# Banded attention with a gated feed-forward: probabilities transposed by VectorE blocks and a DMA round trip instead of TensorE

## The chip, the cores and the metric

The kernel runs on one core of a Trainium2 chip. A core has TensorE (matmuls into PSUM), VectorE (DVE), ScalarE (ACT), GpSimd (POOL), and SyncE (SP), which here issues all DMAs. The metric is device time in microseconds (us), the median over runs of the whole program.

## The reference

Inputs are q, k, v of shape 4 x 8 x 768 x 64 (batch, heads, positions, head size) and four weight matrices. All is float32.

```python
scores = scale * np.matmul(q, k.transpose(0, 1, 3, 2))
rel = pos[:, None] - pos[None, :]
is_global = pos[None, :] < int(n_global)              # 8
is_local = (rel >= 0) & (rel < int(n_local))          # 96
keep = is_global | is_local
dist = np.where(is_global & ~is_local, float(n_local), np.abs(rel))
scores = np.where(keep, scores - slopes * dist, -1000000000.0)
a = softmax(scores)                                   # with 1e-9 added to the sum
attn = np.matmul(a, v)                                # 3072 rows of 512
a = x @ w1                                            # x: attn, heads side by side
b = x @ w2
h = a * b @ w3
out = h @ w_out
```

So each query sees 8 global keys and up to 96 keys behind it, and the result of all heads goes through a gated feed-forward without nonlinearity.

## The kernel before

**Tiling.** The 768 positions of a sequence are cut into 3 blocks of T = 256 rows (`NCB`), 12 blocks in all (`c`), each with two row tiles of 128 (`j`, `NQ` = 2). Heads go in pairs (`hp`, 4 of them; `u` is the head in the pair). A step `s` handles two head pairs of one block (`STEP` = 2), so there are n = 24 steps, two to a block. For one row tile and head the keys are a window of 104 (96 before the tile and the 8 global ones) and the tile's own 128, together 232 columns. On the first block of a sequence the tile j = 0 has no window.

**A step.** `scores` (L406) makes the scores of both pairs in PSUM, 32 small matmuls. `rows` (L421, L422) adds the bias and takes the row maximum on VectorE and does exp with the row sum on ScalarE. `softmax` (L427 to L436) scales the rows by the reciprocal sum, one head on ScalarE, the other on VectorE. `flip` (L445, L447) transposes one row tile's probabilities of both heads on TensorE, four 128x128 transposes against an identity (two where there is no window), and copies the PSUM bank to the tile `ph` on ScalarE (L449); a step has four flips. `values` (L457, L459) multiplies them by v in the next step. `split` (L63, L64) cuts the result into a high and a low part, the tiles `xh` and `xl`, so that the feed-forward can run as three matmuls of the type float32r.

**Feed-forward.** `w3` and `w_out` are multiplied together once at the start (L142). `FeedForward.run` is a generator of slices of about six matmuls of 512 columns (L161 to L163 for the two gates, L178 to L180 for the output). A block of work is appended to the list `work` when its last attention result has been split (blocks 0 and 1 alone, then two blocks together, 48 slices). `slices(k)` emits the next k slices of that list.

**Order.** The order on TensorE and, from step 4 on, on ScalarE is that of the program text; on VectorE and SyncE it is that of the text in steps 0 to 3 only, and the scheduler's after that. From step 4 on a step stands as follows in the text: `visit` (values of the step before, scores of this one, split of the step before), rows, two slices, softmax, the loads of the next step, more slices, and then four flips with slices between them by the table `SLICES`:

```python
SLICES = [()] * 3 + [(4, 2, 2, 1, 1)] * 3 + [(4, 2, 1, 1, 1)] * 2 + [(5, 2, 2, 2, 1)] * (n - 8)
```

**Buffers.** PSUM: the scores have four banks, the flips one, the values one, the feed-forward (`ps_m`) two. `ph` has four buffers of one row tile each, `pr` (probabilities) two, the output tile `ot` two. SyncE issues the loads `qr` (L384) and `vr` (L391) and the stores of the output (L185) in its one queue.

The function `dense` (L207 to L311) is a second path for other band widths, behind a condition; it does not run here.

Of the kernel before, what the change touches and what calls it, by code (L numbers as in the profile page):

```python
# [39 lines left out]
W = 2 * T  # L40
# [20 lines left out]
def split(nc, hi, lo, x):  # L61

    nc.scalar.activation(hi, x, AF.Copy)  # L63
    nc.vector.tensor_tensor(out=lo, in0=x, in1=hi.bitcast(F32), op=ALU.subtract)  # L64
# [142 lines left out]
def dense(ctx, tc, ff, nf, ident, qk, vx):  # L207

    nc = tc.nc
    NB = S // P  # L210
    dr = ctx.enter_context(tc.tile_pool(name="dr", bufs=1, space=bass.MemoryType.DRAM))
    xs = dr.tile([B, NCB, P, NP, T], F32, name="xs")
    with tc.tile_pool(name="dm", bufs=1) as dm, tc.tile_pool(name="dw", bufs=1) as dw, tc.tile_pool(name="dp", bufs=1, space=PSUM) as dp:

        nv = dm.tile([P, 2], F32, name="nv")
        for i in range(2):
            lo, hi = nf[:, 2 * i:2 * i + 1], nf[:, 2 * i + 1:2 * i + 2]
            n = nv[:, i:i + 1]
# [3 lines left out]
        ng, nl = nv[:, 0:1], nv[:, 1:2]  # L222
        far = dm.tile([P, 1], F32, name="far")
        nc.vector.tensor_scalar(out=far, in0=nl, scalar1=0.0, scalar2=None, op0=ALU.max)
        for qb in range(NB):
# [17 lines left out]
            with tc.For_i(0, B, 1) as b:  # L243
                for h in range(H):
                    hp, u = divmod(h, 2)
                    nm = f"{qb}_{h}"
                    src = qk[bass.ds(b, 1), cq, hp, u * D:(u + 1) * D, KW + jq * P:KW + (jq + 1) * P]
                    qd = dw.tile([P, P], F32, tag="qd", name=f"qd_{nm}")
                    kd = dw.tile([P, NB, P], F32, tag="kd", name=f"kd_{nm}")
                    vd = dw.tile([P, NB, D], F32, tag="vd", name=f"vd_{nm}")  # L250
                    for g in range(2):
                        rows = slice(g * D, (g + 1) * D)
                        nc.sync.dma_start(out=qd[rows], in_=src[0])
                        for i in range(NB):
# [5 lines left out]
                    kh = dw.tile([P, NB * P], F32R, tag="kh", name=f"dkh_{nm}")  # L260
                    kl = dw.tile([P, NB * P], F32R, tag="kl", name=f"dkl_{nm}")
                    vs = dw.tile([P, NB, 2, D], F32R, tag="vs", name=f"dvs_{nm}")
# [24 lines left out]
                    ph = dw.tile([P, NB, 2, P], F32R, tag="ph", name=f"dph_{nm}")  # L287
                    for i0 in range(0, NB, 4):
                        i1 = min(i0 + 4, NB)
# [5 lines left out]
                    for i in range(NB):  # L295
                        nc.tensor.matmul(pv, lhsT=vs[:, i], rhs=ph[:, i], start=i == 0, stop=i == NB - 1)
# [28 lines left out]
def banded(ctx, tc, ff, ns, nt, nf, oki, ident, qk, vx):  # L325
# [17 lines left out]
    biasw = bp.tile([P, H, UW], BF16, name="biasw")  # L343

    def biases():
        it = at.tile([P, UW], I32, tag="ph", bufs=4, name="it")
        itg = at.tile([P, P], I32, tag="ph", bufs=4, name="itg")
# [46 lines left out]
    def scores(c, hp, qr):  # L394

        ps = sc[hp % STEP]
        for j in range(NQ):
            w0 = BW if c % NCB == 0 and j == 0 else 0  # L400
            for g in range(P // HQ):
                cols = slice(max(w0, g * HQ), BW + (g + 1) * HQ)
                q0 = KW + j * P + g * HQ
                for u in range(2):
                    m = qr[u * D:(u + 1) * D]
                    nc.tensor.matmul(ps[u][g * HQ:(g + 1) * HQ, j, cols], lhsT=m[:, q0:q0 + HQ], rhs=m[:, j * SLOT:][:, cols], start=True, stop=True)  # L406
        return ps
# [28 lines left out]
                    nc.vector.tensor_scalar(out=x, in0=x, scalar1=r, scalar2=None, op0=ALU.mult)  # L436
        return pr

    def flip(c, hp, j, pr):

        first = c % NCB == 0 and j == 0
        nk = 1 if first else 2
        pt = ps_t.tile([P, 2, 2, P], F32, tag="t", name=f"t_{c}_{hp}_{j}")
        for u in range(2):
            nc.tensor.transpose(pt[:, u, 0], pr[:, j, u, BW:UW], ident)  # L445
            if not first:
                nc.tensor.transpose(pt[:, u, 1], pr[:, j, u, 0:P], ident)  # L447
        ph = at.tile([P, 2, 2, P], F32, tag="ph", bufs=4, name=f"ph_{c}_{hp}_{j}")
        nc.scalar.activation(ph[:, :, :nk], pt[:, :, :nk], AF.Copy)  # L449
        return ph  # L450

    def values(uu, c, hp, vr, phs):
        for j, ph in enumerate(phs):
            first = c % NCB == 0 and j == 0
            for u in range(2):
                rows, o = slice(u * D, (u + 1) * D), uu[u * D:(u + 1) * D, j * P:(j + 1) * P]
                nc.tensor.matmul(o, lhsT=vr[:, j, rows], rhs=ph[:, u, 0], start=True, stop=first)  # L457
                if not first:
                    nc.tensor.matmul(o, lhsT=vr[:BW, 2 * NQ - 1 - j, rows], rhs=ph[:BW, u, 1], start=False, stop=True)  # L459

# [7 lines left out]
    def slices(k):  # L468
        while k > 0 and work:
            if next(work[0], "end") == "end":  # L470
                work.pop(0)
            else:
                k -= 1

    def loads(s, keys=True, vals=True):
        if s < n and keys:
            qrs[s] = [load(*p) for p in pairs(s)]
        if s < n and vals:
            vrs[s] = [load_values(*p) for p in pairs(s)]

    def visit(s):
        if s:
            c, h0 = pairs(s - 1)[0]
            if h0 == 0 and c % 2 == 0:
                xs[c // 2] = [xp.tile([P, NCC, W], F32R, tag=tag, name=f"{tag}_{c}") for tag in ("xh", "xl")]
            uu = ps_v.tile([P, STEP, T], F32, tag="v", name=f"v_{c}_{h0}")
            for i, p in enumerate(pairs(s - 1)):
                values(uu[:, i], *p, vrs[s - 1][i], phs[s - 1][NQ * i:NQ * (i + 1)])
        ps = [scores(*p, t) for p, t in zip(pairs(s), qrs[s])] if s < n else []
        if s:  # L490
            x2 = xs[c // 2]
            xc = [x[:, :, c % 2 * T:][:, :, :T] for x in x2]
            split(nc, *(x[:, h0:h0 + STEP] for x in xc), uu)
            if h0 + STEP == NP and c < 2:
                work.append(ff.run(c, *xc, c * T, T))
            elif h0 + STEP == NP and c % 2:
                work.append(ff.run(c, *x2, (c - 1) * T, W))
        return ps

    def all_rows(s, ps):  # L500
        return [rows(*p, x) for p, x in zip(pairs(s), ps)]

    def turn(s, m, prs):
        phs.setdefault(s, []).append(flip(*pairs(s)[m // NQ], m % NQ, prs[m // NQ][0]))

    def first_steps():

# [94 lines left out]
        fits(nc, ff.mp, nf, oki)  # L602


    SLICES = [()] * 3 + [(4, 2, 2, 1, 1)] * 3 + [(4, 2, 1, 1, 1)] * 2 + [(5, 2, 2, 2, 1)] * (n - 8)
    with tc.manual_schedule(engines={mybir.EngineType.PE}):
        with tc.manual_schedule(engines={mybir.EngineType.DVE, mybir.EngineType.SP}):
            first_steps()
        with tc.manual_schedule(engines={mybir.EngineType.Activation}):
            for s in range(4, n + 1):  # L610
                rs = all_rows(s, visit(s))
                if s == n:
                    break

                slices(2)
                for p, r in zip(pairs(s), rs):
                    softmax(*p, *r, nc.vector)
                loads(s + 1)
                slices(SLICES[s][0] - 2)
                for m in range(STEP * NQ):  # L620
                    turn(s, m, rs)
                    slices(SLICES[s][m + 1])
            slices(10 ** 6)


# [43 lines left out]
```

## Time and profile before

| | |
|---|---|
| median of 3 runs | 600.2 us (599.47 to 601.7) |
| profiled execution: span of its instructions | 597.9 us; of its time outside the span nothing is on record |
| TensorE busy | 574.8 us, 96% |
| VectorE, ScalarE busy | 261.2 us, 287.3 us |
| transposes on TensorE | 192 of L445, 160 of L447 |
| copies of their PSUM bank on ScalarE (L449) | 96, 560 ns each |
| granted TensorE clock, mean | 0.997 |
| DMA | 54.01 MB, mean 90 GB/s |

A row of the groups reads: line, engine, operation, output tile <- input tiles, shapes and count, then busy us and mean ns of one, then the idle time of the engine just before, with what ended it. A row of the timeline reads: start us, duration us, engine, line, operation, tiles, and count where rows are merged. Ends of matmuls are modelled, so starts are the safer reading. In the rows of DMA issues the last number is the median us from issue to landing. In the rows of DMA queues stand packets, MB, and the packets' time as a share of 16 DMA engines over the stretch.

### The profile page before, as it was taken

To read this page: it belongs to the slowest core of one execution; us is meant where nothing else is said; L and a number is where in the kernel's file an instruction comes from. 1 tells how busy PE (TensorE), PEld (TensorE's weight loads), DVE (VectorE), ACT (ScalarE), POOL (GpSimd) and SP (SyncE) were. 2 spreads that over 40 slices of the span, in tenths; PEclk is the share of its full clock that TensorE was granted. 3 is DMA by queue.
4 is the path that set the end of the run, shared out by engine and by line. 5 is a ranking of instruction groups with operands and counts; after the bars stand their busy time and mean duration, and the time that the engine had idled before them with its cause. 6 is when DMAs were issued, how large, how long until landed. Compare 5 with 4: busy or idle time off the path is not lost.

```text
span 597.9 us, 9930 instructions
## 1 busy us (share of the span) xinstructions
PE 574.8 (96%) x3872; PEld 456.3 (76%) x3872; DVE 261.2 (44%) x851; ACT 287.3 (48%) x777; POOL 1.3 (0%) x10
## 2 busy tenths in 40 slices
PE   2998998999999999999999999999999999999995
PEld 0444568989988888888888888888888888888884
DVE  8999998531434425304533322542343453112200
ACT  3065667644556456435635545653553663422210
POOL 0000000000000000000000000000000000000000
PEclk9999999999999999999999999999999999999998
DMA  8896654220132202212211320220331120000011
GB/s 304 296 362 235 218 207 145 81 81 29 52 96 97 77 3 79 81 37 81 79 43 36 115 98 18 62 64 2 123 105 37 42 80 19 36 18 1 0 37 40
DMA packets 23240, 54.01 MB, mean 90 GB/s; under 512 B 2704, under 2 KB 4752, under 8 KB 23184
## 3 DMA queue, kind: packets, MB, share of 16 engines
q1 hardware_dynamic: 23184, 53.29, 26.2%
q8 instruction: 32, 0.52, 0.4%
q14 instruction: 24, 0.20, 0.1%
HBM read 46.99 MB, written 6.29 MB: 89 GB/s over the span
## 4 chain that ended last, share of the span: by engine, by line
PE 84%; DVE 10%; DMA 3%; ACT 1%; issue 0%; SPq 0%; DVEq 0%; ACTq 0%
PE m L161 15%; PE m L163 14%; PE m L162 14%; PE o L178 8%; PE o L180 7%; PE o L179 7%; PE s L406 4%; PE v L457 4%; PE t L445 3%; PE v L459 3%; PE t L447 3%; PE w L142 2%; DVE t L56 1%; DVE t L58 1%; DMA stage<-w3t 1%; DMA raws<-w 1%
## 5 line engine op out<-in xcount | busy, mean ns | idle before, releaser
L422 ACT ACTIVATE pr<-pr,mx 128x232 f32<-128x232 f32 (+1 forms) x192 | 88.4, 462 | 48.1 <-DVE mx L421 48.1
L449 ACT ACTIVATE ph<-t 128x512 f32<-128x512 f32 (+1 forms) x96 | 53.7, 560 | 88.3 <-PE t L447 81.1
L171 DVE TENSOR_TENSOR g<-m,a 128x512 f32<-128x512 f32 x48 | 33.2, 691 | 133.4 <-PE m L163 132.7
L161 PE MATMUL m<-xh,w1h 128*128 128x512 f32 (+1 forms) x224 | 84.5, 377 | 0.0
L161 PE MATMUL m<-xh,w2h 128*128 128x512 f32 (+1 forms) x224 | 83.0, 371 | 0.5 <-ACT a L168 0.5
L163 PE MATMUL m<-xh,w2l 128*128 128x512 f32 (+1 forms) x224 | 80.7, 360 | 0.0
L163 PE MATMUL m<-xh,w1l 128*128 128x512 f32 (+1 forms) x224 | 80.6, 360 | 0.0
L162 PE MATMUL m<-xl,w1h 128*128 128x512 f32 (+1 forms) x224 | 80.5, 360 | 0.0
L162 PE MATMUL m<-xl,w2h 128*128 128x512 f32 (+1 forms) x224 | 80.5, 359 | 0.0
L178 PE MATMUL o<-wh,gh 128*128 128x512 f32 x192 | 78.2, 407 | 0.0
L180 PE MATMUL o<-wh,gl 128*128 128x512 f32 x192 | 75.2, 392 | 0.0
L179 PE MATMUL o<-wl,gh 128*128 128x512 f32 x192 | 75.0, 390 | 0.0
L142 PE MATMUL w<-wo,t 128*128 128x512 f32 x128 | 60.7, 619 | 12.3 <-DVE wo L58 11.2
L64 DVE TENSOR_TENSOR xl<-v,xh 128x512 fp32r<-128x512 f32 x24 | 16.6, 690 | 122.5 <-ACT xh L63 122.5
L63 ACT ACTIVATE gh<-g 128x512 fp32r<-128x512 f32 x48 | 30.3, 630 | 68.0 <-DVE g L171 67.2
L142 PEld LDWEIGHTS w<-wo,t 128*128 128x128 f32 x128 | 24.0, 197 | 39.9 <-issue 21.7
L421 DVE CUSTOM_DVE_ANT_0 pr<-s,biasw 128x232 f32<-128x232 f32 x160 | 53.4, 394 | 0.0
L445 PE MATMUL t<-ident,pr 128*128 128x128 f32 x192 | 45.9, 274 | 4.0 <-ACT pr L434 3.4
L161 PEld LDWEIGHTS m<-xh,w1h 128*128 128x128 f32 x224 | 42.2, 189 | 8.5 <-issue 3.3
L161 PEld LDWEIGHTS m<-xh,w2h 128*128 128x128 f32 x224 | 42.3, 189 | 7.0 <-issue 0.7
L163 PEld LDWEIGHTS m<-xh,w1l 128*128 128x128 f32 x224 | 42.2, 189 | 6.6
L163 PEld LDWEIGHTS m<-xh,w2l 128*128 128x128 f32 x224 | 42.2, 189 | 6.5
(84 smaller groups left out, 807.0 us busy)
## 6 DMA issues: line engine op xcount, KB each, us to landing
qr<-qk SPq DMA_DIRECT2D x32, 312.0 KB, 4.2
vr<-vx SPq DMA_DIRECT2D x32, 256.0 KB, 3.1
stage<-w3t SPq DMA_DIRECT2D x15, 512.0 KB, 6.2
out_dram<-ot SPq DMA_DIRECT2D x24, 256.0 KB, 2.0
raws<-w SPq DMA_DIRECT2D x10, 512.0 KB, 5.6
qr<-qk SPq DMA_DIRECT2D x16, 260.0 KB, 3.5
vr<-vx SPq DMA_DIRECT2D x16, 192.0 KB, 2.6
stage<-w SPq DMA_DIRECT2D x6, 512.0 KB, 6.8
```

The source lines that it names most:

```text
L142: nc.tensor.matmul(ps, lhsT=self.t3[f, z][:, i * P:(i + 1) * P].bitcast(F32), rhs=self.wo[:, k].bitcast(F32), start=k == 0, stop=k == NFC - 1)
L161: nc.tensor.matmul(ps[:, z], lhsT=mh, rhs=xh[:, i], start=i == 0, stop=False)
L162: nc.tensor.matmul(ps[:, z], lhsT=mh, rhs=xl[:, i], start=False, stop=False)
L163: nc.tensor.matmul(ps[:, z], lhsT=ml, rhs=xh[:, i], start=False, stop=i == NCC - 1)
L171: nc.vector.tensor_tensor(out=g, in0=ps, in1=a, op=ALU.mult)
L178: nc.tensor.matmul(ps, lhsT=gh[:, f, ts], rhs=self.wh[:, f], start=f == 0, stop=False)
L179: nc.tensor.matmul(ps, lhsT=gh[:, f, ts], rhs=self.wl[:, f], start=False, stop=False)
L180: nc.tensor.matmul(ps, lhsT=gl[:, f, ts], rhs=self.wh[:, f], start=False, stop=f == NFC - 1)
L421: nc.vector.tensor_tensor_reduce(out=pr[:, j, u, w0:], in0=ps[u][:, j, w0:UW], in1=bias, scale=-SCALE, scalar=3.0e38, op0=ALU.add, op1=ALU ...
L422: nc.scalar.activation(pr[:, j, u, w0:], pr[:, j, u, w0:], AF.Exp, bias=m, scale=-1.0, accum_out=sm[:, j, u:u + 1])
L445: nc.tensor.transpose(pt[:, u, 0], pr[:, j, u, BW:UW], ident)
L449: nc.scalar.activation(ph[:, :, :nk], pt[:, :, :nk], AF.Copy)
```

## The change

From step 4 on (`SWAP`) the probabilities are not transposed on TensorE. After `softmax`, `swap` transposes each 32x32 block by itself on VectorE (four instructions of 128x512 a step), stores the tile of a head pair, 512 KB, to device memory, and `back` reads it again in four DMAs of 128 KB that bring each block to its place; the pieces of these loads are 128 floats long. `values` reads the tile with the block order of that layout. In the first block of a sequence GpSimd clears the part without a window. The PSUM copies of the flips go with the flips. Steps 0 to 3 keep the flips, into a tile for both row tiles; the pool's two buffers of the new tile take the place of four of half the size.

The order on TensorE from step 4 on: scores of the step, then values of the step before, then all slices of the step in one run (`SLICES` now holds one number a step: 10, 9, 9, 8 in steps 4 to 7 where there were 10, 10, 9, 9, then 12 as before). The split of the step before (`take`) stands on ScalarE between the rows of the two head pairs. After the last step the values of step 23 stand ahead of what is left of the slices. The renaming in `dense` (`NB` to `NKB`) changes nothing there.

```diff
+BK = 32
+NB = P // BK
+SWAP = 4
...
+    dr = ctx.enter_context(tc.tile_pool(name="dr", bufs=2 * STEP, space=bass.MemoryType.DRAM))
...
-    def flip(c, hp, j, pr):
+    def flip(c, hp, j, pr, ph):
...
-        ph = at.tile([P, 2, 2, P], F32, tag="ph", bufs=4, name=f"ph_{c}_{hp}_{j}")
-        nc.scalar.activation(ph[:, :, :nk], pt[:, :, :nk], AF.Copy)
-        return ph
+        nc.scalar.activation(ph[:, NQ * j:NQ * j + 2, :nk], pt[:, :, :nk], AF.Copy)
+
+    def swap(c, hp, pr):
+        first = c % NCB == 0
+        x = at.tile([P, 2, NB, NQ * 2, BK], F32, tag="ph", name=f"ph_{c}_{hp}")
+        d = dr.tile([NB, BK, 2, NB, NQ * 2 * BK], F32, tag="d", name=f"d_{c}_{hp}")
+        units = pr.rearrange("p j u k -> p (j u) k")
+        if first:
+            nc.gpsimd.memset(x[:, 1, :, :2], 0.0)
+        for k, k0 in ((0, BW), (1, 0)):
+            u0 = 2 if first and k else 0
+            nc.vector.transpose(x[:, k, :, u0:], units[:, u0:, k0:k0 + P].rearrange("p u (b c) -> p b u c", c=BK))
+        nc.sync.dma_start(out=d.rearrange("a r k b e -> (a r) k b e"), in_=x.rearrange("p k b u c -> p k b (u c)"))
+        return x, d
+
+    def back(x, d):
+        for b in range(NB):
+            nc.sync.dma_start(out=x[b * BK:(b + 1) * BK].rearrange("r k a u c -> r k a (u c)"), in_=d[:, :, :, b].rearrange("a r k e -> r k a e"))
...
-    SLICES = [()] * 3 + [(4, 2, 2, 1, 1)] * 3 + [(4, 2, 1, 1, 1)] * 2 + [(5, 2, 2, 2, 1)] * (n - 8)
+    SLICES = [()] * 3 + [(4, 2, 2, 1, 1)] + [10, 9, 9, 8] + [12] * (n - 8)
...
-            for s in range(4, n + 1):
-                rs = all_rows(s, visit(s))
-                if s == n:
-                    break
-
+            for s in range(4, n):
+                ps = all_scores(s)
+                uu = spread(s - 1)
+                rs = []
+                for i, p in enumerate(pairs(s)):
+                    rs.append(rows(*p, ps[i]))
+                    if i == 0:
+                        take(s - 1, uu)
                 slices(2)
+                loads(s + 1)
+                xd = []
                 for p, r in zip(pairs(s), rs):
                     softmax(*p, *r, nc.vector)
-                loads(s + 1)
-                slices(SLICES[s][0] - 2)
-                for m in range(STEP * NQ):
-                    turn(s, m, rs)
-                    slices(SLICES[s][m + 1])
+                    xd.append(swap(*p, r[0]))
+                for x, d in xd:
+                    back(x, d)
+                phs[s] = [x for x, _ in xd]
+                slices(SLICES[s] - 2)
+            take(n - 1, spread(n - 1))
             slices(10 ** 6)
```

`spread` is the values part of the old `visit`, `take` its split and the appending of feed-forward work, `all_scores` its scores.

More of the change, by code (lines that the diff above doesn't have):

```diff
@@ L209, in dense @@
     nc = tc.nc
-    NB = S // P
-    dr = ctx.enter_context(tc.tile_pool(name="dr", bufs=1, space=bass.MemoryType.DRAM))
+    NKB = S // P
+    dr = ctx.enter_context(tc.tile_pool(name="dx0", bufs=1, space=bass.MemoryType.DRAM))
     xs = dr.tile([B, NCB, P, NP, T], F32, name="xs")
@@ L224, in dense @@
         nc.vector.tensor_scalar(out=far, in0=nl, scalar1=0.0, scalar2=None, op0=ALU.max)
-        for qb in range(NB):
+        for qb in range(NKB):
             cq, jq = divmod(qb, NQ)
@@ L248, in dense @@
                     qd = dw.tile([P, P], F32, tag="qd", name=f"qd_{nm}")
-                    kd = dw.tile([P, NB, P], F32, tag="kd", name=f"kd_{nm}")
-                    vd = dw.tile([P, NB, D], F32, tag="vd", name=f"vd_{nm}")
+                    kd = dw.tile([P, NKB, P], F32, tag="kd", name=f"kd_{nm}")
+                    vd = dw.tile([P, NKB, D], F32, tag="vd", name=f"vd_{nm}")
                     for g in range(2):
@@ L253, in dense @@
                         nc.sync.dma_start(out=qd[rows], in_=src[0])
-                        for i in range(NB):
+                        for i in range(NKB):
                             k0 = BW + i % NQ * SLOT
@@ L259, in dense @@
                     qs = dw.tile([P, P], F32R, tag="qs", name=f"dqs_{nm}")
-                    kh = dw.tile([P, NB * P], F32R, tag="kh", name=f"dkh_{nm}")
-                    kl = dw.tile([P, NB * P], F32R, tag="kl", name=f"dkl_{nm}")
-                    vs = dw.tile([P, NB, 2, D], F32R, tag="vs", name=f"dvs_{nm}")
+                    kh = dw.tile([P, NKB * P], F32R, tag="kh", name=f"dkh_{nm}")
+                    kl = dw.tile([P, NKB * P], F32R, tag="kl", name=f"dkl_{nm}")
+                    vs = dw.tile([P, NKB, 2, D], F32R, tag="vs", name=f"dvs_{nm}")
                     nc.scalar.activation(qs, qd, AF.Copy)
@@ L286, in dense @@
                     nc.vector.tensor_scalar(out=t, in0=t, scalar1=sm, scalar2=None, op0=ALU.mult)
-                    ph = dw.tile([P, NB, 2, P], F32R, tag="ph", name=f"dph_{nm}")
-                    for i0 in range(0, NB, 4):
-                        i1 = min(i0 + 4, NB)
+                    ph = dw.tile([P, NKB, 2, P], F32R, tag="ph", name=f"dph_{nm}")
+                    for i0 in range(0, NKB, 4):
+                        i1 = min(i0 + 4, NKB)
                         pt = dp.tile([P, 4, P], F32, tag="t", name=f"dpt_{nm}_{i0}")[:, :i1 - i0]
@@ L294, in dense @@
                     pv = dp.tile([P, 2, P], F32, tag="v", name=f"dv_{nm}")
-                    for i in range(NB):
-                        nc.tensor.matmul(pv, lhsT=vs[:, i], rhs=ph[:, i], start=i == 0, stop=i == NB - 1)
+                    for i in range(NKB):
+                        nc.tensor.matmul(pv, lhsT=vs[:, i], rhs=ph[:, i], start=i == 0, stop=i == NKB - 1)
                     e = dw.tile([P, P], F32, tag="e", name=f"de_{nm}")
@@ L345, in biases @@
     def biases():
-        it = at.tile([P, UW], I32, tag="ph", bufs=4, name="it")
-        itg = at.tile([P, P], I32, tag="ph", bufs=4, name="itg")
+        it = at.tile([P, UW], I32, tag="ph", name="it")
+        itg = at.tile([P, P], I32, tag="ph", name="itg")
         rel, loc = (at.tile([P, UW], F32, tag="pr", name=n) for n in ("rel", "loc"))
@@ L447, in flip, with values @@
                 nc.tensor.transpose(pt[:, u, 1], pr[:, j, u, 0:P], ident)
-        ph = at.tile([P, 2, 2, P], F32, tag="ph", bufs=4, name=f"ph_{c}_{hp}_{j}")
-        nc.scalar.activation(ph[:, :, :nk], pt[:, :, :nk], AF.Copy)
-        return ph
-    def values(uu, c, hp, vr, phs):
-        for j, ph in enumerate(phs):
+        nc.scalar.activation(ph[:, NQ * j:NQ * j + 2, :nk], pt[:, :, :nk], AF.Copy)
[14 more added lines that the diff above has]
+            nc.sync.dma_start(out=x[b * BK:(b + 1) * BK].rearrange("r k a u c -> r k a (u c)"), in_=d[:, :, :, b].rearrange("a r k e -> r k a e"))
+    def values(uu, c, hp, vr, ph, swapped):
+        for j in range(NQ):
             first = c % NCB == 0 and j == 0
             for u in range(2):
+                m = NQ * j + u
+                own, win = (ph[:, 0, :, m], ph[:BW, 1, :, m]) if swapped else (ph[:, m, 0], ph[:BW, m, 1])
                 rows, o = slice(u * D, (u + 1) * D), uu[u * D:(u + 1) * D, j * P:(j + 1) * P]
-                nc.tensor.matmul(o, lhsT=vr[:, j, rows], rhs=ph[:, u, 0], start=True, stop=first)
+                nc.tensor.matmul(o, lhsT=vr[:, j, rows], rhs=own, start=True, stop=first)
                 if not first:
-                    nc.tensor.matmul(o, lhsT=vr[:BW, 2 * NQ - 1 - j, rows], rhs=ph[:BW, u, 1], start=False, stop=True)
+                    nc.tensor.matmul(o, lhsT=vr[:BW, 2 * NQ - 1 - j, rows], rhs=win, start=False, stop=True)
     n = NC * NP // STEP
@@ L479, in loads, with spread, take, all_scores @@
             vrs[s] = [load_values(*p) for p in pairs(s)]
+    def spread(s):
+        c, h0 = pairs(s)[0]
+        if h0 == 0 and c % 2 == 0:
+            xs[c // 2] = [xp.tile([P, NCC, W], F32R, tag=tag, name=f"{tag}_{c}") for tag in ("xh", "xl")]
+        uu = ps_v.tile([P, STEP, T], F32, tag="v", name=f"v_{c}_{h0}")
+        for i, p in enumerate(pairs(s)):
+            values(uu[:, i], *p, vrs[s][i], phs[s][i], s >= SWAP)
+        return uu
+    def take(s, uu):
+        c, h0 = pairs(s)[0]
+        x2 = xs[c // 2]
+        xc = [x[:, :, c % 2 * T:][:, :, :T] for x in x2]
+        split(nc, *(x[:, h0:h0 + STEP] for x in xc), uu)
+        if h0 + STEP == NP and c < 2:
+            work.append(ff.run(c, *xc, c * T, T))
+        elif h0 + STEP == NP and c % 2:
+            work.append(ff.run(c, *x2, (c - 1) * T, W))
+    def all_scores(s):
+        return [scores(*p, t) for p, t in zip(pairs(s), qrs[s])]
     def visit(s):
+        uu = spread(s - 1) if s else None
+        ps = all_scores(s)
         if s:
[L483 to L497, printed above, removed]
+            take(s - 1, uu)
         return ps
@@ L503, in turn @@
     def turn(s, m, prs):
-        phs.setdefault(s, []).append(flip(*pairs(s)[m // NQ], m % NQ, prs[m // NQ][0]))
+        i, j = divmod(m, NQ)
+        c, hp = pairs(s)[i]
+        if j == 0:
+            phs.setdefault(s, []).append(at.tile([P, NQ * 2, 2, P], F32, tag="ph", name=f"ph_{c}_{hp}"))
+        flip(c, hp, j, prs[i][0], phs[s][i])
     def first_steps():
@@ L609, in banded @@
         with tc.manual_schedule(engines={mybir.EngineType.Activation}):
-            for s in range(4, n + 1):
-                rs = all_rows(s, visit(s))
-                if s == n:
-                    break
+            for s in range(4, n):
+                ps = all_scores(s)
+                uu = spread(s - 1)
+                rs = []
+                for i, p in enumerate(pairs(s)):
+                    rs.append(rows(*p, ps[i]))
+                    if i == 0:
+                        take(s - 1, uu)
                 slices(2)
+                loads(s + 1)
+                xd = []
                 for p, r in zip(pairs(s), rs):
                     softmax(*p, *r, nc.vector)
-                loads(s + 1)
-                slices(SLICES[s][0] - 2)
-                for m in range(STEP * NQ):
-                    turn(s, m, rs)
-                    slices(SLICES[s][m + 1])
+                    xd.append(swap(*p, r[0]))
[4 more added lines that the diff above has]
+            take(n - 1, spread(n - 1))
             slices(10 ** 6)
```

## The prediction

> **What bounds the kernel now.** I read the page first: the busy shares, the clock row, the chain that ended last.
>
> ```profile
> span 597.9 us, 9930 instructions
> PE 574.8 (96%) x3872; PEld 456.3 (76%) x3872; DVE 261.2 (44%) x851; ACT 287.3 (48%) x777; POOL 1.3 (0%) x10
> PEclk9999999999999999999999999999999999999998
> PE 84%; DVE 10%; DMA 3%; ACT 1%; issue 0%; SPq 0%; DVEq 0%; ACTq 0%
> PE m L161 15%; PE m L163 14%; PE m L162 14%; PE o L178 8%; PE o L180 7%; PE o L179 7%; PE s L406 4%; PE v L457 4%; PE t L445 3%; PE v L459 3%; PE t L447 3%; PE w L142 2%; DVE t L56 1%; DVE t L58 1%; DMA stage<-w3t 1%; DMA raws<-w 1%
> ```
>
> TensorE is 96% busy at full clock and 84% of the ending chain; the rest is the weight stage at the start. From step 4 on nothing else ends a wait that matters. So PE time taken out comes off the end, unless a new wait opens. Then the timeline of TensorE gives the period of a step (score matmuls to score matmuls) and its parts:
>
> ```profile
> 309.46 0.71 PE L457 MATMUL v<-ph,vr 128*64 128x128 f32 x8
> 310.98 1.37 PE L406 MATMUL s<-qr 64*64 64x168 f32 x32
> 312.28 0.50 PE L161 MATMUL m<-xh,w1h 128*128 128x512 f32 x1
> ...
> 332.71 1.37 PE L406 MATMUL s<-qr 64*64 64x168 f32 x32
> ```
>
> ```profile
> 311.00:332.70 21.70, 21.70 (x153) 17.84 (x152) 8.49 (x30) 11.34 (x30) 0.00 (x0) 1.00 0.19 61
> ```
>
> The last row is that stretch in the view by windows: busy time of PE, PEld, DVE, ACT and POOL, then clock and DMA. TensorE is busy in all of it, VectorE 8.5 us, ScalarE 11.3. The period is 332.71 - 310.98 = 21.73 us: values 1.5 us (309.46 to 310.98), scores 1.3 us, the rest is twelve feed-forward slices and four flips.
>
> **What is removed.** Matmul ends are modelled, so I price a flip by starts, not durations:
>
> ```profile
> 509.66 0.39 PE L180 MATMUL o<-wh,gl 128*128 128x512 f32 x1
> ...
> 512.38 0.39 PE L180 MATMUL o<-wh,gl 128*128 128x512 f32 x1
> 512.61 0.27 PE L445 MATMUL t<-ident,pr 128*128 128x128 f32 x1
> 512.72 0.27 PE L447 MATMUL t<-ident,pr 128*128 128x128 f32 x1
> ...
> 512.97 0.48 PE L178 MATMUL o<-wh,gh 128*128 128x512 f32 x1
> 513.28 0.39 PE L179 MATMUL o<-wl,gh 128*128 128x512 f32 x1
> ...
> 515.82 0.27 PE L445 MATMUL t<-ident,pr 128*128 128x128 f32 x1
> ...
> 519.01 0.27 PE L445 MATMUL t<-ident,pr 128*128 128x128 f32 x1
> ```
>
> Twelve undisturbed matmuls take 512.38 - 509.66 = 2.72 us (0.227 each). A flip and twelve matmuls take (519.01 - 512.61)/2 = 3.20. So a flip costs 0.48 us: four transposes 0.11 apart, then a slow first matmul (0.31 to the next instead of 0.23). Steps 4 to 23 have 80 flips; in the six steps on the first block of a sequence (6, 7, 12, 13, 18, 19) the j = 0 flips, 12 in all, hold two transposes, 0.48 - 2 x 0.11 = 0.26. Removed: 68 x 0.48 + 12 x 0.26 = 35.7 us, all on the bound engine. The period falls to 21.73 - 4 x 0.48 = 19.8 us.
>
> ScalarE loses the PSUM copies below, four a step. It is not the bound: no gain by itself.
>
> ```profile
> L449 ACT ACTIVATE ph<-t 128x512 f32<-128x512 f32 (+1 forms) x96 | 53.7, 560 | 88.3 <-PE t L447 81.1 <-PE t L445 7.1
> L64 DVE TENSOR_TENSOR gl<-g,gh 128x512 fp32r<-128x512 f32 x48 | 33.2, 692 | 31.9 <-ACT gh L63 31.9
> L54 DVE TENSOR_SCALAR t<-stage 128x512 int32<-128x512 int32 x15 | 5.8, 417 | 0.5 <-PE w L142 0.5
> L63 ACT ACTIVATE gh<-g 128x512 fp32r<-128x512 f32 x48 | 30.3, 630 | 68.0 <-DVE g L171 67.2
> ```
>
> **What is added.** VectorE gets four block transposes of 128x512 a step. No row shows one; the nearest of that size are 0.42 us (one source) and 0.69 us (two sources). I take 0.69, since a shuffle across lanes is unlikely to beat a plain pass: 2.8 us a step. With its 8.5 us it has room; the cost is latency. The GpSimd clear on first blocks stands beside TensorE's work: nothing. SyncE gets ten DMAs a step (two stores of 512 KB, eight loads of 128 KB).
>
> The round trip is a new wait of the value matmuls. Time from the first score matmul of a step, by these rows:
>
> ```profile
> 312.33 0.39 DVE L421 CUSTOM_DVE_ANT_0 pr<-s,biasw 128x232 f32<-128x232 f32 x1
> 314.56 0.39 DVE L421 CUSTOM_DVE_ANT_0 pr<-s,biasw 128x232 f32<-128x232 f32 x1
> 312.82 0.49 ACT L422 ACTIVATE pr<-pr,mx 128x232 f32<-128x232 f32 x1 [1.13 <-DVE mx L421]
> 316.14 0.47 ACT L422 ACTIVATE pr<-pr,mx 128x232 f32<-128x232 f32 x1
> 317.09 1.62 ACT L434 ACTIVATE pr<-pr,sm 128x232 f32<-128x232 f32 x4
> ```
>
> Maxima are 0.32 apart ((314.56 - 312.33)/7), exps 0.47 apart. Scores end at 1.3, values at about 3.0. The first pair's maxima start at about 1.0, its exps run 1.5 to 3.4; then `take`'s copy, 0.6, waits for the values and ends at 4.0; the second pair's exps end at 5.9. Two slices end on TensorE at 3.0 + 12 x 0.227 = 5.7; if the second closes a feed-forward block, its product (0.69) and copy (0.63) stand next on ScalarE until about 7.2. The scalings take 1.6: first pair done 8.0, second 8.8. Two transposes each: 9.4 and 10.8. Behind them:
>
> ```profile
> out_dram<-ot SPq DMA_DIRECT2D x24, 256.0 KB, 2.0
> stage_xl<-w3t SPq DMA_DIRECT2D x1, 512.0 KB, 10.0
> DMA packets 23240, 54.01 MB, mean 90 GB/s; under 512 B 2704, under 2 KB 4752, under 8 KB 23184
> L185 SPq DMA_DIRECT2D out_dram<-ot x24: 332/343/344, 127.8 to 592.4; - x24
> q1 hardware_dynamic: 576, 1.05, 4.5%
> q1 hardware_dynamic: 3876, 11.35, 78.8%
> ```
>
> The last two rows are the DMA view of two stretches, 535 to 598 us (stores in 2 KB packets) and 20 to 60 us (mostly loads in 4 KB packets). They give 4.5% x 16 x 63 / 1.05 = 43 and 78.8% x 16 x 40 / 11.35 = 44 us of one engine per MB: time goes with bytes. A 256 KB store lands in 2.0 us, of which 0.7 moves data; 512 KB then takes 2.7. The other end is the 10.0 of a load in the crowded first stage; at this point of a step the queue is empty, so I take 2.7. Writes land at 12.1 and 13.5. The loads come in 512 B pieces, 64 per engine and pair. By bytes a piece takes 22 ns; the upper end is the price of a whole 2 KB packet, 4.5% x 16 x 63 us / 512 = 88 ns. As time has gone with bytes I take 28: 1.8 us a pair. SyncE issues each in 0.34, eight from 12.1 to 15.0; with the 1.3 that a store spends beside moving data, the last lands at 16.5 to 17.5. Values are next due at 19.8 + 1.3 = 21.1. Slack about 4 us: hidden.
>
> Queues: stores to the output sit behind the round trip on SyncE; they have two buffers and no reader, so nothing. The next loads are issued ahead of it. `take` moved between the pairs' exps delays the high half of x by about 1 us; the two slices that steps 5 and 7 now leave over stand ahead of each new group (2.7 us) and cover that.
>
> Two exposed costs remain. The early steps are short:
>
> ```profile
> 166.12 1.24 PE L406 MATMUL s<-qr 64*64 64x64 f32 x32
> 182.76 1.37 PE L406 MATMUL s<-qr 64*64 64x168 f32 x32
> L445 PEldq EVENT_SEMAPHORE  x10: 51/51/51, 36.0 to 508.6; - x10
> ```
>
> Step 7 takes 16.64 us; less its flips (2 x 0.48 + 2 x 0.26 = 1.5) and one slice (1.4), 13.8. Its values are due at 15.1, the round trip lands at about 16.5: 1.5 us late, once. The other early steps are within 1 us of fitting. And TensorE must now await several DMAs where it awaited one copy: some three added waits a step at 51 ns, 0.15 us, 3 us in 20 steps (bounds 0 and eight waits, 8 us).
>
> Sum on the profiled execution: 597.9 - 35.7 + 1.5 + 3.0 = 566.7 us of span. The median of the runs shown, 600.2, is 2.3 above that span; so 569.
>
> **The rivals.**
> *Slower: small packets are priced by count.* At 88 ns a 512 B piece, both pairs need 128 x 88 ns = 11.3 us per DMA engine, from 13.4 on: ready at 24.7, 3.6 us late every step, 72 us in 20 steps: 641 us. It turns into a loss where the lateness exceeds 35/20 = 1.75 us, that is from about 74 ns a piece. For it: hardly a data piece this small was moved here (the 2704 packets under 512 B are nearly all semaphore writes, sixteen to a DMA; the next are 4752 - 2704 = 2048 of the loads of 192 KB, 1.5 KB each). Against it: 43 and 44 us per MB at different packet sizes. The Trainium skill ("DMA: Bandwidth & Descriptors", Rules for kernel authors) warns that a plain DMA with a rearranged access pattern is 19 times slower as a transpose than the hardware's own; by that factor on the 1.8 us, an estimate, each pair would need 34 us and the kernel would pass 1,500 us. Here 128 floats stay together in each piece, so I give that little weight, and no run so far shows it.
>
> On such waits the clock bears too: the row above shows it granted in full throughout. The Trainium skill ("TensorE: Matmul & The Clock Gate", Part 1) says that some 3.4 us without activity halve the clock; if the 3.6 us waits did that, an estimate of 1.7 us more a step would make this rival 675 us. The trace has no such gap late in the run.
>
> *Partly hidden.* VectorE takes `take`'s subtraction ahead of the second pair's maxima (+1.2 us), a transposition waits behind a feed-forward product (+0.7), or an output store awaiting ScalarE stands ahead of the loads on SyncE (up to 5). For it: the orders of VectorE and SyncE from step 4 on are the scheduler's, which this trace cannot show. A lateness of 0.5 to 1 us a step gives 579 to 589.
>
> *No change* needs 1.75 us lateness by chance. Another engine as the bound I rule out: VectorE 8.5 + 2.8 = 11.3 us of 19.8, ScalarE less than before.
>
> **How the numbers follow.** Hidden, 562 to 576: 0.65. Partly hidden, 576 to 597: 0.20. Within 0.5% (about what a measurement of this kernel can tell from no change): 0.03. Slower: 0.12. The range, 561 to 592, holds the first and most of the second. Faster: 0.85.
>
> **What would show it.** Right: L445, L447 and L449 left with steps 0 to 3 alone; periods of score matmuls near 19.8 us; no TensorE wait on the DMA into `ph` beyond step 8; transposes near 0.69 us; the loads landing 2 to 3 us after issue. Wrong: a gap ahead of L457's successor in every period, ended by that DMA, with a longer period and perhaps a lower clock; or transposes of several us.

## The result, and the profile after

The changed kernel takes 577.4 us (median of 4 runs, 576.5 to 579.3) against 600.0 for the kernel before: ratio 0.962, interval 0.960 to 0.965. It is 8.4 us above the predicted 569.0 and 1.4 above the top of the range given to the likeliest case, though inside the whole range; it falls in the bracket 576 to 597 of "partly hidden", which had a chance of 0.20. The profiled execution has a span of 574.7 us against 597.9. The medians below leave out two slow executions, one of 691.2 us at a mean granted clock of 0.757 and one of 604.3 us.

From the page of the changed kernel, its busy shares, clock row, chain, the group of the block transposes and the DMA issues (KB each, median us to landing):

```profile
span 574.7 us, 9856 instructions
PE 544.5 (95%) x3576; PEld 429.9 (75%) x3576; DVE 307.9 (54%) x931; ACT 243.6 (42%) x697; POOL 5.1 (1%) x22
PEclk9999899999997999999999999999999999999999
PE 70%; DVE 11%; DMA 8%; SPq 4%; ACT 4%; issue 2%; DVEq 0%; ACTq 0%
L466 DVE STREAM_TRANSPOSE ph<-pr 128x512 f32<-128x512 f32 x80 | 46.6, 640 | 9.1 <-ACT pr L438 5.6 <-issue 2.9
d<-ph SPq DMA_DIRECT2D x40, 512.0 KB, 2.7
ph<-d SPq DMA_DIRECT2D x160, 128.0 KB, 3.2
```

TensorE lost 30 us of modelled busy time. New in the chain that ended last are DMA (8%, before 3%) and SyncE's queue, SPq (4%, before 0%): in some stretch the round trip sets the end. The clock row shows where: a 7 in the thirteenth of its forty slices, 172 to 187 us (the 8 ahead of it is in the weight stage). The waits of the value matmuls say how much (us in total, times, longest; the larger waits of other matmuls were there before):

```profile
PE v L481 <- DMA ph<-d: 5.0, 5, 2.6
...
PE v L481 <- DVE sm L431: 2.2, 1, 2.2
```

The first is the round trip. The second belongs to it too: the instruction on `sm` that it names is part of the next softmax, which these values do not read, and the kernel without the trip (below) has no such wait. Together 7.2 us, all before step 12; the steps behind it have none. The timeline and the windows view (busy PE, PEld, DVE, ACT, POOL, then clock, DMA share, GB/s) of one step there:

```profile
320.82 1.37 PE L410 MATMUL s<-qr 64*64 64x168 f32 x32
...
340.66 1.37 PE L410 MATMUL s<-qr 64*64 64x168 f32 x32
320.82:340.66 19.84, 19.84 (x137) 16.28 (x136) 7.53 (x29) 7.78 (x24) 0.00 (x0) 1.00 0.66 203
```

The period is 19.84 us, all of it busy and at full clock. Step 8 looks different (TensorE, then SyncE's queue, then its stretches):

```profile
175.90 1.37 PE L410 MATMUL s<-qr 64*64 64x168 f32 x32
179.51 0.68 PE L481 MATMUL v<-ph,vr 128*64 128x128 f32 x8 [2.25 <-DVE sm L431]
182.97 1.15 PE L481 MATMUL v<-ph,vr 128*64 128x128 f32 x8 [2.56 <-DMA ph<-d]
185.49 0.63 PE L183 MATMUL o<-wh,gl 128*128 128x512 f32 x1
185.92 0.63 PE L181 MATMUL o<-wh,gh 128*128 128x512 f32 x1
...
202.48 1.37 PE L410 MATMUL s<-qr 64*64 64x168 f32 x32
```

```profile
171.17 1.60 SPq L467 DMA_DIRECT2D d<-ph  x2
...
174.39 5.67 SPq L472 DMA_DIRECT2D ph<-d  x8
```

```profile
177.40:180.82 3.42, 0.90 (x12) 0.69 (x12) 2.84 (x18) 1.84 (x8) 0.00 (x0) 1.00 0.75 184
180.82:184.23 3.41, 1.26 (x12) 1.20 (x12) 0.00 (x0) 0.00 (x0) 0.00 (x0) 0.50 0.96 298
184.23:187.64 3.41, 3.41 (x12) 2.52 (x9) 1.18 (x4) 2.47 (x9) 0.00 (x0) 0.50 0.24 84
187.64:191.05 3.41, 3.41 (x16) 2.82 (x15) 1.08 (x3) 2.06 (x5) 0.00 (x0) 1.00 0.18 67
```

The eight loads are issued from 174.39 to 180.06 (5.67 us), so TensorE waits for the first pair's probabilities until 179.51 and for the second pair's until 182.97. From 180.82, early in the second wait, to 187.64 the granted clock is 0.50, and TensorE works at it for 1.26 + 3.41 = 4.7 us: matmuls start 0.43 apart (185.49 to 185.92) instead of 0.23. The step takes 26.58 us (175.90 to 202.48).

### The profile page after: what moved, and what is told of

Read it like the earlier page. It is cut to its first block, busy times and chain, and to the rows that moved or that the text cites. A ratio compares the mean times of both kernels' runs of the same rounds, so it can differ in the third digit from the quotient of the medians.

```text
span 574.7 us, 9856 instructions
## 1 busy us (share of the span) xinstructions
PE 544.5 (95%) x3576; PEld 429.9 (75%) x3576; DVE 307.9 (54%) x931; ACT 243.6 (42%) x697; POOL 5.1 (1%) x22
## 4 chain that ended last, share of the span: by engine, by line
PE 70%; DVE 11%; DMA 8%; SPq 4%; ACT 4%; issue 2%; DVEq 0%; ACTq 0%
PE m L164 12%; PE m L165 12%; PE m L166 12%; PE o L181 7%; PE o L182 6%; PE o L183 6%; SPq L472 4%; PE v L481 4%; PE w L145 4%; PE s L410 3%; DMA ph<-d 3%; DMA d<-ph 3%; PE v L483 2%; ACT pr L426 2%; DVE t L59 1%
## 5 line engine op out<-in xcount | busy, mean ns | idle before, releaser
L164 PE MATMUL m<-xh,w2h 128*128 128x512 f32 (+1 forms) x224 | 81.7, 365 | 0.2 <-ACT a L171 0.2
L164 PE MATMUL m<-xh,w1h 128*128 128x512 f32 (+1 forms) x224 | 80.8, 361 | 0.0
L181 PE MATMUL o<-wh,gh 128*128 128x512 f32 x192 | 76.7, 400 | 0.0
L145 PE MATMUL w<-wo,t 128*128 128x512 f32 x128 | 61.9, 630 | 13.2 <-DVE wo L61 11.2
L466 DVE STREAM_TRANSPOSE ph<-pr 128x512 f32<-128x512 f32 x80 | 46.6, 640 | 9.1 <-ACT pr L438 5.6
L67 DVE TENSOR_TENSOR gl<-g,gh 128x512 fp32r<-128x512 f32 x48 | 33.2, 692 | 32.3 <-ACT gh L66 32.3
L171 ACT ACTIVATE a<-m 128x512 f32<-128x512 f32 x48 | 28.5, 593 | 45.6 <-PE m L166 45.6
L165 PEld LDWEIGHTS m<-xl,w1h 128*128 128x128 f32 x224 | 42.3, 189 | 6.3
```

Source lines behind the costliest of these rows:

```text
L145: nc.tensor.matmul(ps, lhsT=self.t3[f, z][:, i * P:(i + 1) * P].bitcast(F32), rhs=self.wo[:, k].bitcast(F32), start=k == 0, stop=k == NFC - 1)
L164: nc.tensor.matmul(ps[:, z], lhsT=mh, rhs=xh[:, i], start=i == 0, stop=False)
L165: nc.tensor.matmul(ps[:, z], lhsT=mh, rhs=xl[:, i], start=False, stop=False)
L181: nc.tensor.matmul(ps, lhsT=gh[:, f, ts], rhs=self.wh[:, f], start=f == 0, stop=False)
L466: nc.vector.transpose(x[:, k, :, u0:], units[:, u0:, k0:k0 + P].rearrange("p u (b c) -> p b u c", c=BK))
```

## The experiments

Spans below are those of the profiled executions; times are medians, ratios are to the kernel before. A step's period runs from its first score matmul to the next step's. The parts of the span are told by such periods.

**What is the round trip worth at all?** The store and the loads are left out.

```diff
-        nc.sync.dma_start(out=d..., in_=x...)
...
-                for x, d in xd:
-                    back(x, d)
```

> The store to device memory and the eight loads are left out (the blocks stay where VectorE put them, so the output is not the reference's); all else stays. Theory: the whole distance from 577.4 us to my 569 is the round trip coming late in the short early steps; TensorE waited 7.3 us on it (2.25 + 2.56 of them at step 8) and lost about 2 us more to the lower clock behind that wait. So 577.4 - 9 = 568 us, step 8 down from 26.6 to 19.9 us, granted clock in full there. Rival: the loss at step 8 is the change of feed-forward width and the moved split, not the trip: 575 to 577 us and step 8 stays above 24 us.

565.0 us, ratio 0.942 (0.941 to 0.944), span 562.6, no wait of TensorE on `ph`. Taking the flips off TensorE is worth 597.9 - 562.6 = 35.3 us; the round trip gives 574.7 - 562.6 = 12.1 back. By steps (before, changed, without the trip; us, from unrounded starts):

| step | before | changed | no trip |
|---|---|---|---|
| 1 | 22.16 | 23.93 | 22.27 |
| 5 | 19.65 | 17.49 | 16.16 |
| 6 | 17.47 | 17.16 | 16.27 |
| 7 | 16.64 | 14.69 | 13.94 |
| 8 | 21.73 | 26.58 | 19.37 |
| 11 | 21.72 | 20.29 | 19.85 |
| 15, 16 | 21.72 | 19.85 | 19.85 |

So 3.0 us are lost in steps 5 to 7, 7.2 in step 8, 0.4 in step 11, together 10.6; the remaining 1.5 stand almost all in the first four steps (step 1), where no round trip runs yet. Of step 8's 7.2, the two waits are 2.25 + 2.56 = 4.8; the other 2.4 are the half clock, since 4.7 us of work at half the clock cost 2.3.

**Is it the early steps?** Step 7 alone goes back to TensorE's flips.

```diff
+    FLIPS = {7: (4, 1, 1, 1, 1)}
...
+                if s in FLIPS:
+                    ...
+                    for m in range(STEP * NQ):
+                        turn(s, m, rs)
+                        slices(FLIPS[s][m + 1])
+                    continue
```

> Step 7 alone, the shortest (14.7 us), transposes on TensorE again, with its flips between its slices as before. Theory: only the values of step 7 come badly late; without their trip step 8 falls from 26.6 to about 20 us (-6.7), for 1.5 us of flips in step 7: 572 us. Rival (the loss belongs to step 8 itself): 578 to 579 us.

571.9 us, ratio 0.953 (0.951 to 0.955), span 570.1. As expected: step 8 falls to 19.36 us, step 7 rises to 16.11, steps 5 and 6 stay late (17.28, 16.98), and the clock dip of step 8 is gone:

```profile
175.00:200.00 25.00, 25.00 (x206) 20.40 (x204) 12.80 (x48) 12.14 (x36) 0.00 (x0) 1.00 0.53 169
```

**Is SyncE's issue the limit?** In the changed kernel an issue of a load into `ph` takes 0.61 us (min, median, max in ns):

```profile
L472 SPq DMA_DIRECT2D ph<-d x160: 557/611/1637, 121.8 to 494.7; - x160
```

Starts are 0.64 apart, 5.15 us for eight. One kernel puts both pairs into one tile and reads it in four loads of 256 KB.

```diff
-            nc.sync.dma_start(out=x[b * BK:(b + 1) * BK]... "r k a u c -> r k a (u c)", in_=d[:, :, :, b] ...)
+            nc.sync.dma_start(out=x[b * BK:(b + 1) * BK]... "r i k a u c -> r i k a (u c)", in_=d[:, :, :, :, b] ...)
...
+                back(x, d)     # once a step, behind the stores of both pairs
```

> Both head pairs share one tile and one buffer in device memory, so the loads are four of 256 KB instead of eight of 128 KB; bytes and piece length are the same. Theory: SyncE issues a load in 0.64 us, so eight cost 5.2 us of a trip of 11.8 and four cost 2.6; the last load then starts some 2.6 us earlier. Step 8 would lose 5.7 - 2.6 = 3 us instead of 6.7, steps 5 to 7 nothing: 571 to 573 us. Rival: the moving of 512 B pieces is what takes the time (1024 pieces an engine row whatever the count of DMAs): the last landing stays where it was and the time is 576 to 578 us.

601.0 us, ratio 1.001 (0.999 to 1.004), span 599.1. A miss: half as many issues made it 24 us slower than the changed kernel.

```profile
PE v L478 <- DMA ph<-d: 25.2, 14, 7.9
...
329.11 1.51 SPq L465 DMA_DIRECT2D d<-ph  x2
333.15 2.60 SPq L469 DMA_DIRECT2D ph<-d  x4
...
ph<-d SPq DMA_DIRECT2D x80, 256.0 KB, 5.2
```

The issue fell to 2.60 us as intended. But the first load now awaits both stores, so it starts 333.15 - 329.11 = 4.0 us after the first store's issue (changed kernel: 332.54 - 329.89 = 2.65), and a load lands 5.2 us after its issue instead of 3.2. The packets of 512 B took 48 ns each (median), against 27 in the changed kernel. The loads of the first pair no longer run beside the second pair's work. The edit changed two things at once, and the number of issues is not the whole limit.

**The same bytes in large pieces.** The loads keep their number, size, queue and waits, but read 32 rows of 4 KB.

```diff
-... x[b * BK:(b + 1) * BK].rearrange("r k a u c -> r k a (u c)"), in_=d[:, :, :, b].rearrange("a r k e -> r k a e")
+... x[b * BK:(b + 1) * BK].rearrange("r k a u c -> r (k a u c)"), in_=d[b].rearrange("r k a e -> r (k a e)")
```

> The four loads of a pair read 32 rows of 4 KB in one piece instead of 256 pieces of 512 B; the blocks then land in the wrong places, so the values are not those of the reference; bytes, queue, number of loads and all waits stay. Theory: the number of pieces sets both the 0.61 us of one issue on SyncE and the 3.2 us to landing. Issue about 0.33 us as for the store, eight in 2.9 us, landing 2.0 to 2.5, so the last lands some 3 us earlier; steps 5 to 7 are then in time and step 8 keeps about 1.5 us: 566 to 569. Rival: an issue of a load of this size takes 0.61 us whatever its pieces, or the wait is for the store's completion: 575 to 578, unchanged.

571.1 us, ratio 0.951 (0.950 to 0.953), span 569.5: 6.3 us faster than the changed kernel, but not the 566 to 569 expected.

```profile
L472 SPq DMA_DIRECT2D ph<-d x160: 308/419/1367, 120.9 to 488.1; - x160
ph<-d SPq DMA_DIRECT2D x160, 128.0 KB, 3.1
...
175.55 0.73 PE L481 MATMUL v<-ph,vr 128*64 128x128 f32 x8 [2.13 <-DVE mx L425]
178.13 1.15 PE L481 MATMUL v<-ph,vr 128*64 128x128 f32 x8 [1.42 <-DMA ph<-d]
...
172.64:176.05 3.41, 1.28 (x33) 1.00 (x27) 3.08 (x19) 2.00 (x8) 0.00 (x0) 1.00 0.95 243
176.05:179.47 3.42, 2.00 (x20) 1.46 (x15) 0.42 (x2) 0.00 (x0) 0.00 (x0) 0.50 0.93 286
```

Half of the theory holds: an issue falls from 0.61 to 0.42 us, eight start within 3.57 instead of 5.15, and steps 5 to 7 take 16.16, 16.27 and 13.94 us, those of the kernel without a trip. So the pieces cost SyncE's time, and that time was the 3.0 us of these steps. The other half falls: 3.1 us to landing in place of 3.2. That time does not come from the pieces; what makes it is open. Step 8 still has two waits and the half clock (25.63 us), which here starts at 176.05, behind the first wait and ahead of the second.

**Is there a cliff?** Every load is issued twice.

```diff
-        for b in range(NB):
+        for b in [*range(NB)] * 2:
```

> Every load of the trip is issued twice. Theory: the steady steps hide the trip with only 0.5 to 1.8 us to spare (last landing 19.3 to 20.6 us into a step, due at 21.1), so 5.2 us more on SyncE makes every step from 4 on 3.4 to 4.7 us late: 577 + 19 x 4 = 653 us, and 20 to 35 us more if the clock falls behind each wait as it did at step 8. Rival (my forecast's slack of 4 us): 1 to 1.5 us a step, 600 to 607 us.

724.7 us, ratio 1.208 (1.202 to 1.215). The direction is the expected one, the size some 70 us more than expected, and more than the clock's 20 to 35 allowed for. TensorE waited 107.9 us on the loads in 27 waits (without the clock in that figure), and the clock fell in nearly every step (mean 0.898 against 0.99). The expectation also left out that lateness is passed on: the second pair's exps stand behind `take` on ScalarE, which awaits the late values, and in the step at 398.62 the stores are issued from 415.25, 16.6 us into the step instead of 9.07. The slack of the changed kernel is therefore small against the time of eight more loads.

```profile
PE v L481 <- DMA ph<-d: 107.9, 27, 6.5
PEclk9999999789769889798989889889899889889999
415.25 1.50 SPq L467 DMA_DIRECT2D d<-ph  x2
```

**What is the new order worth?** Two kernels: the new order with TensorE's flips in all steps and no round trip; and the round trip with values ahead of scores.

```diff
+    FLIPS = {4: (4, 2, 2, 1, 1), ..., 7: (4, 1, 1, 1, 1)} | {s: (5, 2, 2, 2, 1) for s in range(8, n)}
```

> The new order (scores, values, split between the rows of the two pairs, shorter early steps) with TensorE's flips in every step; no block transposes, no trip. Theory: the order by itself moves nothing, 599 to 601 us, so that the whole gain is the flips' 35 us less the late trip. Rival: the order gives part of the gain: 590 to 596 us.

599.9 us, ratio 1.000 (0.999 to 1.001): by itself the order is worth nothing.

```diff
+                uu = spread(s - 1)
                 ps = all_scores(s)
-                uu = spread(s - 1)
```

> Scores no longer stand ahead of values; all else stays. The values of a step are then due at 19.85 - 1.6 = 18.25 us after its score matmuls, instead of 21.15. Theory (last landing at 18.6 to 20.6 us, by the start of the first load plus 7.7): nearly every step is 0.4 to 2.3 us late, some 1.5 on average, and step 8 another 2.9: 577 + 19 x 1.5 + 3 = 600 to 610 us, that is the whole gain. Rival (slack of 4 us, as forecast): 577 to 585 us.

594.5 us, ratio 0.991 (0.988 to 0.993), span 592.1. Less lost than my theory had it, more than the rival. With the trip the order is worth 592.1 - 574.7 = 17.4 us: values due 1.3 us earlier leave many steps late.

```profile
PE v L481 <- DMA ph<-d: 19.1, 14, 3.5
```

**Values later.** In every step both pairs' rows and two slices stand ahead of the values; in a second kernel, step 7's flips besides.

```diff
-                uu = spread(s - 1)
-                rs = []
-                for i, p in enumerate(pairs(s)):
-                    rs.append(rows(*p, ps[i]))
-                    if i == 0:
-                        take(s - 1, uu)
+                rs = all_rows(s, ps)
                 slices(2)
+                uu = spread(s - 1)
+                take(s - 1, uu)
```

> In the steps from 4 on two slices stand on TensorE between the scores and the values, and ScalarE does the rows of both pairs before the split. Values are due 2.7 us later, at about 23.9 us in full steps. Theory: the waits of steps 5 to 7 and 11 (3.4 us) go, of step 8 (7.2 us with the clock behind it) at most 2 to 3 us stay, as only two slices are left over there: 566 to 570 us. Rival (the moved split makes the feed-forward wait at the four group starts): 2 us each, 574 to 578 us.

> The same, and step 7 transposes on TensorE. Theory: no late trip is left: 565.0 (the kernel without the trip) + 1.5 us of flips = 566 to 568 us. Rival: waits of the trip stay elsewhere, 570 us or more.

571.8 us (0.954, 0.952 to 0.956) and 573.4 us (0.955, 0.953 to 0.956): between my theory and the rival, and worse than expected for the second. Its trace has no TensorE wait on the round trip left, and yet its span is 9.0 us above that without a trip. The periods say why. Steps 5 to 7 of the first take 16.40, 16.45 and 14.13 us, so the lateness there is gone, but every later step is 0.24 longer:

```profile
313.75 1.37 PE L410 MATMUL s<-qr 64*64 64x168 f32 x32
333.85 1.37 PE L410 MATMUL s<-qr 64*64 64x168 f32 x32
```

That is 20.10 instead of 19.84, busy all the while: TensorE changes once more from large to small matmuls and back. In its step 8 the first feed-forward matmul behind the scores holds the next one for 0.34 us (174.07 to 174.41) and the first value matmul starts 0.32 behind the last of the feed-forward (176.74 to 177.06), both instead of 0.23, which makes 0.2 of the 0.24. In steps 9 to 22 this is 278.9 against 275.5 us, 3.4 us for nothing. The rest of the second kernel's 9.0 us: 2.5 in steps 4 to 8 (1.6 of it step 7 with its flips), 0.8 in the first four steps (step 1's clock, see below), and 2.2 behind the start of step 23, where TensorE's work is the same and the last store ends later.

**Later only where it is late.** Steps 4 to 8 alone get the later values; the second kernel asks for a third slice ahead of them in step 8.

```diff
+                late = 2 if s <= 8 else 0        # second kernel: 3 if s == 8
+                if late:
+                    rs = all_rows(s, ps)
+                    slices(late)
                 uu = spread(s - 1)
+                if late:
+                    take(s - 1, uu)
...
```

> The later values (rows of both pairs, two slices, then the values of the step before) in steps 4 to 8 only; from step 9 on the order of the changed kernel. Theory: the later order costs 0.24 us in every step in which the trip was in time anyway (20.09 against 19.85 us, two more switches between small and large matmuls) and gains only in steps 5 to 8. Steps 9 to 22 fall back to 275.5 us together from 278.9, so 3.4 us less than with the later order everywhere: span 566.6, time about 569 (567.5 to 570.5). Rival: without the later order the loads of steps 9 to 22, which have 0.5 to 1.8 us to spare, are late again in some steps: 571 to 576.

> As the kernel with the later values in steps 4 to 8, but three slices ahead of them in step 8, where the trip of step 7 still made TensorE wait 1.75 us. Theory: a third slice (1.6 us) covers that wait: 1.6 us less than the two-slice version, about 567.5 (566 to 569). Rival: the rows and the split of step 8 then run later, and what was won goes to a later write (issued 10.7 us into step 8 already): no difference, or slower.

569.2 us (0.949, 0.947 to 0.951) and 569.8 us (0.951, 0.949 to 0.952), spans 567.3 and 566.8. The first is as expected (569, span 566.6) and beats both kernels: 8.2 us less than the changed one. Steps 5 to 7 keep 16.40, 16.45 and 14.13, and the period is back:

```profile
PE v L481 <- DMA ph<-d: 2.3, 2, 1.8
...
313.44 1.37 PE L410 MATMUL s<-qr 64*64 64x168 f32 x32
333.29 1.37 PE L410 MATMUL s<-qr 64*64 64x168 f32 x32
...
176.41:179.82 3.41, 1.83 (x17) 1.10 (x15) 1.86 (x10) 2.30 (x9) 0.00 (x0) 1.00 0.75 222
237.49 0.45 PE L481 MATMUL v<-ph,vr 128*64 128x128 f32 x4 [0.57 <-DMA ph<-d]
```

The window is in its step 8: a single long wait of 1.8 us, and the clock stays at 1.00. The last row is the other wait, in step 11, which takes 20.62 us instead of 19.85: there the rival came, in that one step.

The third slice did nothing, and not for the reason given by the rival. At that place the list of work held two slices only, since the next block is appended by the very `take` behind it. The trace has twelve matmuls ahead of the values of step 8 in both kernels and a wait of 1.8 us in both; the edit only moved one slice out of step 8 to the end. So step 8 cannot be covered this way.

## Why the prediction was right or wrong

**Flips, right.** 35.7 us predicted, 35.3 measured by the kernel without the trip. The period was to be 19.8 and is 19.84. Pricing a flip by starts, the slow next matmul included, held; busy time would have given 30.

**Block transposes, right.** 0.69 us taken, 0.64 measured.

**Stores, right.** Issue predicted 9.4 and 10.8 us after the first score matmul of the step; in the step at 320.82 they are issued at 9.07 and 10.26 (median landing 2.7, as predicted).

**A 512 B piece, right.** 28 ns taken, 27 measured, so the rival "small packets are priced by count" (88 ns) did not come. Nor did the estimate of 34 us a pair, made from the 19-fold difference that the Trainium skill ("DMA: Bandwidth & Descriptors", Rules for kernel authors) gives between a plain DMA with a rearranged access pattern and the hardware's own transpose: both pairs come back within a period of 19.84 us. No run here used the hardware's transpose, so the difference itself is not tested. Four loads of 256 KB at a time made a piece 48 ns, so the 28 is a price for loads that stand apart.

**Issue and landing of the loads, wrong. This is the step that failed.** "SyncE issues each in 0.34, eight from 12.1 to 15.0; with the 1.3 that a store spends beside moving data, the last lands at 16.5 to 17.5 [...] Slack about 4 us." Issues take 0.61 and start 0.64 apart, so the last of eight starts 4.5 us behind the first instead of some 2.5; it lands 3.2 us after issue, where moving its data and 1.3 us make about 1.75. In the step at 320.82 the queue shows this:

```profile
329.89 1.51 SPq L467 DMA_DIRECT2D d<-ph  x2
332.54 5.15 SPq L472 DMA_DIRECT2D ph<-d  x8
```

Loads begin 11.7 us into the step; the last starts at about 16.2 and lands at about 19.4 by the median of the run, at 19.8 by the 3.6 us of these eight, against 21.1 due. Slack in this step is 1.3 to 1.7 us by the prediction's own count, not 4. (That count takes the first value matmul as due; the last load serves the second pair, whose value matmuls start 0.9 us later, 342.90 against 341.96.) It differs from step to step, and step 10 has none: that is the 0.4 us in step 11. Both prices came from a store of whole rows (0.34 us to issue, 2.0 to land), although the page of before had loads:

```profile
vr<-vx SPq DMA_DIRECT2D x32, 256.0 KB, 3.1
...
vr<-vx SPq DMA_DIRECT2D x16, 192.0 KB, 2.6
```

By these, 128 KB had 2.6 to 3.1 us to land, and the slack would have come out near 3. The issue time of a load in many pieces stood in no row; the prediction should have kept an end above 0.34 for it. Why a load needs more than moving its data and 1.3 us is not shown by any run.

**Exposed early steps, right in place and wrong in size.** Predicted: step 7's trip late by 1.5 us once, the others "within 1 us of fitting". Measured: 3.0 us in steps 5 to 7, 7.2 in step 8 (which waits for step 7's trip), 0.4 in step 11, 10.6 in all. With some 2.5 us off the assumed slack this follows roughly, the half clock in step 8 (2.4 us) excepted. The prediction weighed the clock only for a wait in every step.

**Added semaphore waits.** 3.0 us were charged; without the trip the span is 562.6 where 597.9 - 35.7 = 562.2, and late steps have the same period with and without the trip (19.85). None is seen in steady steps.

**The sum.** 566.7 us of span predicted, 574.7 measured: +0.4 flips, +9.1 late trips (10.6 for 1.5), -3.0 waits that did not come, and 1.5 outside the steps with a trip make +8.0. The 3.0 us charged for nothing hid a part of the late trips; that is luck. The last item is mostly step 1 (23.93 us against 22.16). It is not the trip's: the kernel with the new order and no trip took 23.37 there, and the one with the later values and the third slice, with the trip, 21.87. It is the clock, in a stage where TensorE waits for weights; 3.41 us of work at half the clock cost 1.7:

```profile
57.94:61.35 3.41, 1.36 (x5) 0.70 (x5) 3.34 (x11) 2.71 (x7) 0.00 (x0) 1.00 0.44 143
61.35:64.76 3.41, 3.41 (x8) 1.71 (x7) 3.41 (x7) 1.72 (x6) 0.00 (x0) 0.50 0.95 376
```

These rows are of the changed kernel. Of the thirteen traces, the eight with such a stretch at half clock have a step 1 of 22.9 to 23.9 us, the five without it one of 21.9 to 22.7. Which trace has it is chance: it hangs on where the clock's 3.41 us stretches fall, as the last section shows.

**The rivals.** "Partly hidden" gave 579 to 589 for 0.5 to 1 us in every step, by extra VectorE and SyncE order. The time came just below its lower end, but by another way: no lateness in most steps, several us in five early ones. "Slower by small packets" had the wrong price but the right consequence: the doubled loads and the four large ones show that a trip past its slack costs at least that lateness in most steps, with the clock on top.

## What to carry to other kernels

A round trip through device memory can hide work moved off a bound engine, but its slack must be worked out step by step: the shortest step decides, since there the trip is as long and the cover is not. Price a load from the landing of loads, not of stores, and its issue from DMAs with as many pieces; where a queue issues many, count starts, not only bytes. Move the consumer later only in the steps that are late: elsewhere the extra change between kinds of matmul costs 0.24 us a step and buys nothing.

## What the runs showed of the hardware

- SyncE's time to issue a DMA differed with its pieces: 0.61 us for 128 KB in 256 pieces of 512 B, 0.42 for the same bytes in 32 pieces of 4 KB, 0.33 for the store of 512 KB. Landing did not follow: 3.2 and 3.1 us.
- The granted clock goes by stretches of 3.41 us, not by the length of a wait. In each of the thirteen traces it changes only at times that lie a whole number of 3.41 us apart, as at 61.35, 180.82 and 187.64 in the changed kernel, and the grid lies differently in each trace. A stretch at full clock in which TensorE was busy for 1.37 us or less (0.40 of it) was followed by half the clock in all thirteen traces, one with 1.47 us or more (0.43) never. In the kernel with large pieces a wait of 2.13 us left 1.28 us of a stretch busy, and the clock fell; in the one with four loads a step a wait of 3.42 us in step 5 lay across two stretches, and the clock stayed:

```profile
131.31 0.45 PE L478 MATMUL v<-ph,vr 128*64 128x128 f32 x4 [3.42 <-DMA ph<-d]
126.03:129.45 3.42, 1.86 (x35) 1.20 (x33) 2.08 (x13) 2.17 (x8) 0.00 (x0) 1.00 1.21 189
129.45:132.86 3.41, 1.55 (x28) 1.58 (x30) 1.42 (x8) 0.42 (x2) 0.00 (x0) 1.00 0.89 263
132.86:136.27 3.41, 3.41 (x22) 2.75 (x18) 1.04 (x3) 2.92 (x11) 0.00 (x0) 1.00 0.40 115
```

  The Trainium skill ("TensorE: Matmul & The Clock Gate", Why this matters for your kernels) advises against idle gaps beyond about 3 us between bursts of matmuls. The traces differ from that advice both ways: the gap of 2.13 us cost the clock and the one of 3.42 us did not.
- A 32 by 32 block transpose of 128x512 float32 on VectorE takes 0.64 us, about as long as a pass with two sources.
